# A planned retention and mixture kernel: new durations in its planner, one load on another queue, other bursts and other filler

## The chip, the core and the metric

One Trainium2 chip, of which the kernel uses one core. The metric is the device time of one execution in microseconds (us). Five engines work side by side, each through its own instructions in order: TensorE (PE in the profile, its weight loads PEld), VectorE (DVE), ScalarE (ACT), GpSimd (POOL) and SyncE (SP), which here only issues transfers. An instruction that waits holds up all behind it on its engine.

## The reference

Eight batches of eight heads, 576 positions, 64 values per head. Retention (attention without a softmax, with a decay per head) and then two dense layers with a leaky ReLU between them:

```python
scores = scale * np.matmul(q, k.transpose(0, 1, 3, 2))
gamma = 1.0 - 2.0 ** (-5.0 - np.arange(H, dtype=np.float32))
Dmat = np.where(rel >= 0, gamma[:, None, None] ** rel[None, :, :], 0.0)
attn = np.matmul(scores * Dmat[None], v)
x = attn.transpose(0, 2, 1, 3).reshape(4608, 512)
h = x @ w_in                 # 512 x 2048
out = np.maximum(0.01 * h, h) @ w_out   # 2048 x 512
```

## The kernel before

**Units.** The 4608 tokens are cut into 36 units of 128 tokens, two chunks of 64 each. For unit u, `load` (L619) brings k, q and v as 128 x 8 x 64 float32 (jobs `ld{u}.1`, `.0`, `.2`). `casts` (L641) makes float16: k is copied (`ck`, L648), q and v are multiplied by the decay (`cq`, `cv`: L652 on DVE or POOL, L656 as eight small instructions on ACT). q and k are transposed, for units 0 to 7 by PE with a copy from PSUM (`turn_pe`, L686 and L693), later by a transposing transfer on SP's queue (`turn_dma`, L672).

**Retention.** `inner` (L710) computes the scores within a chunk (`sa`, L721), the mask (`mk`, DVE, L736), the states k^T v (`sb`, L730), their running sums (`st`, DVE, L779 to L785) and the sums in float16 (`sx`, L799 and L802). `outer_mm` (L838) multiplies scores by v (own part) and states by q (cross part) into the PSUM tile `ot` (L842); a copy turns it into x (`x{u}`, L891). All these matmuls are 64 x 64 and run on quarters of the array. They come in three forms: units 0 to 3 (below `drain`) in separate jobs, with a drain of PE between own and cross part (L903); units from 4 to below `joined`, `parted`, as two short bursts (cross part and scores, job `ca{u}`; states and own part, jobs `sb{u}` and `ow{u}`); all later ones as one long burst (`bu{u}`, L755), which also holds the own part of the unit before.

**Dense layers.** Four units make a group of 512 tokens, nine groups. Groups 0 to 2 take layer 1 as it is (`layer1`, L947 with leaky ReLU on ACT, L954); its blocks need quarters of w_in (four loads `wi0` to `wi3`, L921). All others, and layer 2 everywhere, use a scheme of seven products instead of eight (`seven`, L1048, a variant of Strassen's): layer 1 at L1128, layer 2 at L1204, with sums on DVE (L1108 `xs`, L1182 `mix`, L1150, L1237) and copies of PSUM on ACT or DVE (L1073 `cA`, L1078 `u2`, L1081 `k5`). The weights' mixtures (L995, L1024) are formed once on DVE. The output leaves by SP's queue (L1039, L1240).

**What sets the order.** Nothing is issued as it is written. Every step becomes a job with an engine, two durations in ns (how long it keeps the engine, and when its result is there), the jobs it waits for and the buffers it opens. `Plan.order` (L120) then plays the machine on the host: it takes again and again the job that can begin first, among those that can begin within `slack` the one with the earliest due time, and so fixes each engine's order. The durations stand in the table `COST` (L589), in `BURST`, in `SWITCH` (what PE loses at each change between 64 x 64 and full matmuls) and in the `add` calls; when a load lands is modelled, and four early landings are given by hand (`landing`). Which engine takes a copy stands in tables (`engines`, `eng`), and due times are shifted job by job in two more (`nudge`, `shift_due`).

**Filler.** Where the planner sees PE idle before a job, `filler` (L1296) puts matmuls of zeros (`idle`, 512 columns, L1304) into PE's order, counted by the planned length of the gap. They are ordinary instructions: they run whether or not PE is late.

**Loads.** POOL's queue issues units 1 to 11, w_in and w_out; SP's queue unit 12 and later. Unit 0's k and q go by SP, its v by POOL, ahead of w_in. A POOL load takes POOL's own time to issue (about 0.9 us), and a POOL order holds casts as well. In the built order a queue has eight semaphores in turn, so the ninth transfer is issued when the first has landed.

Of the kernel before, what the change touches and what calls it, by code (L numbers as in the profile page):

```python
# [46 lines left out]
class Plan:  # L47
# [3 lines left out]
    SWITCH = 115  # L51
# [68 lines left out]
    def order(self, margin=30, slack=30, filler=None):  # L120
        self.urgency(margin)
        jobs = self.jobs
# [55 lines left out]
        while todo:  # L178
# [12 lines left out]
            if best is None:  # L191
                raise RuntimeError("no job can begin: " + ", ".join(
                    f"{j.name}({','.join(a.name for a in j.after if a.end is None)};{j.follow.name if j.follow and j.follow.start is None else ''})"
                    for j in jobs if j.start is None and (j.name[0] in 'ab')))
# [56 lines left out]
def _cfg():  # L251
# [28 lines left out]
            "cv0 sx0.0 yt2.1 sx2.1 sx3.1 cv4 yt4.0 sx5 sx7 sx11 sx12 cq13 cv16 sx19 sx21 sx25 cq26 cv27 cv30 "  # L280
            "sx30 sx31 sx32 sx35 ",
        "DVE":
# [4 lines left out]
        "POOL":  # L287
            "ck3 cv7 cv8 cq10 cv10 cv11 sx13 cv17 sx18 ck19 ck20 ck24 sx24 ck26 sx27 sx28 ck29 cq29 sx29 ck31 "
            "ck32 cv32 ck33 cv33 sx33 cv34 sx34 cv35 ",
    }  # L290
    nudge = {
        -10026:
            "cv29 ",
        -10724:
            "h0.12.384 ",
        -10966:
            "mk4 ",
        -11853:
            "xs4.2 ",
        -11976:  # L300
            "a3.2.k5 ",
        -12515:
            "b3.21 ",
        -128684:
            "a6.3.p2.0 ",
        -14832:
            "h2.4.256 ",
        -15153:
            "m3.1.0 ",
        -15169:  # L310
            "mk23 ",
        -15592:
            "ld18.0 ",
        -19363:
            "ca4 ",
        -2236:
            "sx3.0 ",
        -251919:
            "cv1 ",
        -2689:  # L320
            "m1.2.1 ",
        -293979:
            "b8.p1.1 ",
        -31306:
            "h0.12.0 ",
        -40696:
            "sx2.0 ",
        -429774:
            "a8.3.p7.0 ",
        -653:  # L330
            "m4.2.0 ",
        -8008:
            "xs5.2 ",
        -837:
            "mk26 ",
        -8459:
            "mk34 ",
        -8774:
            "ld21.2 ",
        -9071:  # L340
            "m3.2.1 ",
        11277:
            "tr22 ",
        12355:
            "st33.0 ",
        14015:
            "ld29.0 ",
        15252:
            "xs7.2 ",
        15629:  # L350
            "mk29 ",
        15684:
            "xs5.3 ",
        18754:
            "ld14.1 ",
        18924:
            "h1.10.256 ",
        21497:
            "m5.0.0 ",
        23022:  # L360
            "b5.p4.0 ",
        28841:
            "ld26.0 ",
        3776:
            "m3.3.1 ",
        3956:
            "mk21 ",
        3958:
            "m3.0.0 ",
        5404:  # L370
            "st32.0 ",
        5601:
            "m3.2.0 ",
        5647:
            "b0.p1.0 ",
        6624:
            "m5.1.1 ",
        7138:
            "x29 ",
        7265:  # L380
            "st24.0 ",
        8339:
            "so2.1 ",
        8675:
            "bu31 ",
    }
    shift_due = {
        -12686:
            "b1.p1.0 b1.p1.1 b1.cA b1.p2.0 b1.p2.1 b1.11 b1.p6.0 b1.p6.1 b1.u2 b1.p5.0 b1.p5.1 b1.k5 b1.p7.0 "
            "b1.p7.1 b1.22 b1.p3.0 b1.p3.1 b1.12 b1.p4.0 b1.p4.1 b1.21 ",  # L390
        -14351:
            "l1.6.0 l1.6.256 ",
        -166113:
            "h2.2.0 h2.2.256 ",
        -16905:
            "b3.p1.0 b3.p1.1 b3.cA b3.p2.0 b3.p2.1 b3.11 b3.p6.0 b3.p6.1 b3.u2 b3.p5.0 b3.p5.1 b3.k5 b3.p7.0 "
            "b3.p7.1 b3.22 b3.p3.0 b3.p3.1 b3.12 b3.p4.0 b3.p4.1 b3.21 ",
        -179758:
            "h1.0.0 h1.0.256 ",
        -20648:  # L400
            "b0.p1.0 b0.p1.1 b0.cA b0.p2.0 b0.p2.1 b0.11 b0.p6.0 b0.p6.1 b0.u2 b0.p5.0 b0.p5.1 b0.k5 b0.p7.0 "
            "b0.p7.1 b0.22 b0.p3.0 b0.p3.1 b0.12 b0.p4.0 b0.p4.1 b0.21 ",
        -26677:
            "l1.4.0 l1.4.256 ",
        -26684:
            "a6.0.p1.0 a6.0.cA a6.0.p2.0 a6.0.11 a6.0.p6.0 a6.0.u2 a6.0.p5.0 a6.0.k5 a6.0.p7.0 a6.0.22 "
            "a6.0.p3.0 a6.0.12 a6.0.p4.0 a6.0.21 ",
        -28444:
            "x16 ",
        -29807:  # L410
            "l3.3.22 l3.3.12 ",
        -30711:
            "a4.2.p1.0 a4.2.cA a4.2.p2.0 a4.2.11 a4.2.p6.0 a4.2.u2 a4.2.p5.0 a4.2.k5 a4.2.p7.0 a4.2.22 "
            "a4.2.p3.0 a4.2.12 a4.2.p4.0 a4.2.21 ",
        -31154:
            "a5.1.p1.0 a5.1.cA a5.1.p2.0 a5.1.11 a5.1.p6.0 a5.1.u2 a5.1.p5.0 a5.1.k5 a5.1.p7.0 a5.1.22 "
            "a5.1.p3.0 a5.1.12 a5.1.p4.0 a5.1.21 ",
        -31278:
            "a7.0.p1.0 a7.0.cA a7.0.p2.0 a7.0.11 a7.0.p6.0 a7.0.u2 a7.0.p5.0 a7.0.k5 a7.0.p7.0 a7.0.22 "
            "a7.0.p3.0 a7.0.12 a7.0.p4.0 a7.0.21 ",  # L420
        -31546:
            "a5.0.p1.0 a5.0.cA a5.0.p2.0 a5.0.11 a5.0.p6.0 a5.0.u2 a5.0.p5.0 a5.0.k5 a5.0.p7.0 a5.0.22 "
            "a5.0.p3.0 a5.0.12 a5.0.p4.0 a5.0.21 ",
        -31652:
            "a4.1.p1.0 a4.1.cA a4.1.p2.0 a4.1.11 a4.1.p6.0 a4.1.u2 a4.1.p5.0 a4.1.k5 a4.1.p7.0 a4.1.22 "
            "a4.1.p3.0 a4.1.12 a4.1.p4.0 a4.1.21 ",
        -36269:
            "a4.0.p1.0 a4.0.cA a4.0.p2.0 a4.0.11 a4.0.p6.0 a4.0.u2 a4.0.p5.0 a4.0.k5 a4.0.p7.0 a4.0.22 "
            "a4.0.p3.0 a4.0.12 a4.0.p4.0 a4.0.21 ",
        -37687:  # L430
            "x27 ",
        -39781:
            "l5.2.22 l5.2.12 ",
        -44863:
            "xs7.0 xs7.1 xs7.2 xs7.3 ",
        -45803:
            "a6.2.p1.0 a6.2.cA a6.2.p2.0 a6.2.11 a6.2.p6.0 a6.2.u2 a6.2.p5.0 a6.2.k5 a6.2.p7.0 a6.2.22 "
            "a6.2.p3.0 a6.2.12 a6.2.p4.0 a6.2.21 ",
        -46221:
            "h0.4.0 h0.4.128 h0.4.256 h0.4.384 ",  # L440
        -53848:
            "l4.3.22 l4.3.12 ",
        -65535:
            "l3.0.22 l3.0.12 ",
        -6965:
            "b7.p1.0 b7.p1.1 b7.cA b7.p2.0 b7.p2.1 b7.11 b7.p6.0 b7.p6.1 b7.u2 b7.p5.0 b7.p5.1 b7.k5 b7.p7.0 "
            "b7.p7.1 b7.22 b7.p3.0 b7.p3.1 b7.12 b7.p4.0 b7.p4.1 b7.21 ",
# [970 lines left out]
```

## Time and profile before

| | |
|---|---|
| median of three runs | 292.39 us (290.34, 292.39, 293.9) |
| the profiled execution | 290.67 us, of which the span from first to last instruction is 288.9 us |
| mean granted PE clock | 0.994 of full speed |
| DMA | 50.08 MB, mean 173 GB/s; share of the 16 engines 1.1 and more in most stretches until 200 us, 0.22 and less from 200 to 270 |
| POOL L652 (multiplies of q and v) | 38, mean 1057 ns (q) and 1125 ns (v) |
| DVE L652 (multiplies of q) | 18, mean 756 ns |
| DVE L1182 (mixtures) | 72, means 682 to 788 ns by form |
| DVE L1150 and L1237 (sums with one operand in PSUM) | 66, means 683 to 688 ns |
| filler matmuls | 36 |

A row of the profile names engine, line, operation, the tile written and the tiles read, the count, and busy time with the mean of one. In a timeline a row begins with its start and length in us; in square brackets stands the idle time just before it and what ended it. A row of the stretches gives the stretch, its length, the busy time of PE, PEld, DVE, ACT and POOL with counts, then the granted PE clock, the DMA share and GB/s. Matmuls overlap, so their lengths add up to more than the time they take: distances from start to start are the better measure.

### The profile page before, as it was taken

What the parts mean: (1) busy time and instruction counts of PE and PEld (TensorE: products, weight loads), DVE (VectorE), ACT (ScalarE), POOL (GpSimd) and SP (SyncE); (2) the same over time, 40 slices, a digit from 0 to 9 for tenths busy, and PEclk for the clock granted to TensorE, in tenths of its full rate; (3) what the DMA queues carried; (4) which work ended last, traced back from release to release, by engine and by line L of the source; (5) the groups of instructions that cost most, each with busy time, mean ns of one, the idle gap of its engine ahead of it and who ended that gap; (6) DMA issues with size and microseconds to landing.
All of it is one profiled execution on the core that took longest, in us unless ns stands there. A gap on an engine that the chain in (4) does not pass through costs nothing.

```text
span 288.9 us, 10486 instructions
## 1 busy us (share of the span) xinstructions
PE 277.2 (96%) x4532; PEld 233.3 (81%) x4532; DVE 215.4 (75%) x385; ACT 182.1 (63%) x366; POOL 94.3 (33%) x111
## 2 busy tenths in 40 slices
PE   8979999999999999999899999999999999999994
PEld 3559978888878888887788888888888888888883
DVE  1575777998986798877998889889958963872541
ACT  3515987543657857775595789778755755566630
POOL 8867996743141233323321412354010000000000
PEclk9989999999999999999999999999999999999999
DMA  7996999999999999999999999999401100300303
GB/s 160 288 233 144 281 209 235 324 196 173 188 278 222 210 197 218 262 205 236 231 223 242 204 269 215 183 221 217 69 3 75 74 2 0 149 0 2 149 0 145
DMA packets 119247, 50.08 MB, mean 173 GB/s; under 512 B 107936, under 2 KB 112672, under 8 KB 119200
## 3 DMA queue, kind: packets, MB, share of 16 engines
q1 hardware_dynamic: 111856, 36.19, 59.9%
q0 software_dynamic: 7056, 13.11, 19.3%
q8 instruction: 35, 0.57, 0.9%
q10 hardware_dynamic: 288, 0.11, 0.2%
q14 instruction: 12, 0.10, 0.1%
HBM read 36.81 MB, written 9.44 MB: 160 GB/s over the span
## 4 chain that ended last, share of the span: by engine, by line
PE 70%; DVE 9%; DMA 9%; SPq 6%; issue 3%; POOL 1%; ACT 1%; ACTq 0%; DVEq 0%; POOLq 0%
PE acc L1204 29%; PE acc L1128 20%; PE acc L947 13%; DMA w_in<-in_moe_w_in_dram 6%; SPq L627 5%; PE ot L842 4%; DMA t<-in_k_dram 2%; DVE s L736 2%; PE sc L730 2%; DMA t<-in_q_dram 1%; DVE w_mix L995 1%; PE sc L721 1%; SPq L672 1%; DVE mix L1182 1%; DVE sum L1150 1%
## 5 line engine op out<-in xcount | busy, mean ns | idle before, releaser
L1204 PEld LDWEIGHTS <-gt 128*128 128x128 f16 x720 | 69.5, 98 | 8.4
L1204 PE MATMUL acc<-w_out,gt 128*128 128x256 f16 x432 | 54.8, 273 | 0.0
L947 PE MATMUL acc<-xT,w_in 128*128 128x128 f16 (+1 forms) x512 | 48.3, 251 | 1.9 <-DMA w_in<-in_moe_w_in_dram 1.3
L947 PEld LDWEIGHTS <-w_in 128*128 128x128 f16 x512 | 40.0, 100 | 5.9 <-issue 1.8
L1128 PEld LDWEIGHTS <-w_in 128*128 128x128 f16 x384 | 36.4, 98 | 7.3 <-issue 2.4
L1155 ACT ACTIVATE gt<-sum 128x512 f16<-128x512 f32 x48 | 29.7, 628 | 19.4 <-DVE sum L1150 19.4
L954 ACT ACTIVATE gt<-acc 128x512 f16<-128x512 f32 x48 | 28.3, 597 | 17.7 <-PE acc L947 17.6
L1146 ACT ACTIVATE gt<-acc 128x512 f16<-128x512 f32 x48 | 28.5, 594 | 13.7 <-PE acc L1128 13.3
L1204 PE MATMUL acc<-w_mix,gt 128*128 128x256 f16 x288 | 36.0, 273 | 0.0
L652 POOL TENSOR_TENSOR v<-t,cs 128x512 f16<-128x512 f32 x22 | 24.7, 1125 | 25.1 <-DMA t<-in_v_dram 10.3
L652 POOL TENSOR_TENSOR qk<-t,cs 128x512 f16<-128x512 f32 x16 | 16.9, 1057 | 48.9 <-PE sc L730 17.5
L736 DVE TENSOR_TENSOR s<-sc,cs 128x512 f16<-128x512 f32 x36 | 24.7, 686 | 9.8 <-PE sc L721 6.6
L1204 PEld LDWEIGHTS <-mix 128*128 128x128 f16 x288 | 27.7, 98 | 4.2 <-issue 0.6
L1128 PEld LDWEIGHTS <-w_sum 128*128 128x128 f16 x288 | 27.6, 98 | 4.1 <-DVE xs L1108 0.8
L1128 PE MATMUL acc<-xs,w_in 128*128 128x256 f16 x192 | 28.9, 273 | 1.0 <-DVE sum L1150 1.0
L1128 PE MATMUL acc<-xs,w_sum 128*128 128x256 f16 x192 | 28.9, 273 | 0.5 <-DVE xs L1108 0.5
L1128 PE MATMUL acc<-xT,w_in 128*128 128x256 f16 x192 | 28.9, 273 | 0.5 <-DVE acc L1073 0.3
L1150 DVE TENSOR_TENSOR sum<-acc,k 128x512 f32<-128x512 f32 x24 | 16.5, 688 | 10.0 <-ACT k L1081 5.9
L1081 ACT COPY k<-acc 128x512 f32<-128x512 f32 x28 | 16.4, 589 | 7.9 <-PE acc L1128 4.1
L781 DVE TENSOR_TENSOR s<-sc,s 128x256 f32<-128x256 f32 x40 | 16.7, 418 | 4.0 <-PE sc L730 2.1
L652 DVE TENSOR_TENSOR qk<-t,cs 128x512 f16<-128x512 f32 x18 | 13.6, 756 | 8.1 <-DMA t<-in_q_dram 7.3
L1073 ACT COPY acc<-acc 128x512 f32<-128x512 f32 x26 | 15.0, 577 | 7.2 <-PE acc L1204 4.0
(68 smaller groups left out, 461.8 us busy)
## 6 DMA issues: line engine op xcount, KB each, us to landing
out_dram<-osb SPq DMA_DIRECT2D x17, 512.0 KB, 4.0
t<-in_k_dram SPq DMA_DIRECT2D x22, 256.0 KB, 4.7
t<-in_q_dram SPq DMA_DIRECT2D x22, 256.0 KB, 4.5
t<-in_v_dram SPq DMA_DIRECT2D x21, 256.0 KB, 4.8
t<-in_v_dram POOLq DMA_DIRECT2D x11, 256.0 KB, 6.3
t<-in_k_dram POOLq DMA_DIRECT2D x10, 256.0 KB, 7.4
t<-in_q_dram POOLq DMA_DIRECT2D x10, 256.0 KB, 6.6
w_in<-in_moe_w_in_dram POOLq DMA_DIRECT2D x8, 256.0 KB, 8.3
```

What stands on the lines that cost most here:

```text
L652: engine[e].tensor_tensor(out=out, in0=t32[u, 2 * x][:], in1=decay(u, x), op=MUL)
L736: landed[u] = nc.vector.tensor_tensor(out=s[:], in0=a[:, :, 0], in1=mask_sb.unsqueeze(1).unsqueeze(1).to_broadcast([P, 2, NP, CH]), op=MUL,)
L781: nc.vector.tensor_tensor(out=to, in0=x, in1=before[0][:, before[1]], op=ADD)
L947: nc.tensor.matmul(out=a[:, n, :], lhsT=w_in16[:, c, (f0 + n) * P : (f0 + n + 1) * P], rhs=x[:, c, t0 : t0 + nt], start=(n == 0 and c == 0 ...
L954: nc.scalar.activation(out=y[:, f0 : f0 + nf, t0 : t0 + nt], in_=a[:], func=mybir.ActivationFunctionType.Lrelu)
L1073: op("cA", ce, lambda: copies[ce](out=B[:], in_=A[:]), [done["1"]], [B], [A], "1")
L1081: op("k5", ke, lambda: copies[ke](out=k5[:], in_=C[:]), [done["5"]], [k5], [C], "5")
L1128: nc.tensor.matmul(out=r[:, f, :], lhsT=w[:, c, (2 * n + f) * P : (2 * n + f + 1) * P], rhs=rhs[:, c, :], start=fresh and c == 0 and f == ...
L1146: w = op(what, "ACT", lambda: nc.scalar.activation(out=to(), in_=r[:], func=lr), after, [y], [r], m)
L1150: what, "DVE", lambda: nc.vector.tensor_tensor(out=s[:], in0=r[:], in1=plus[:], op=ADD),
L1155: lambda: nc.scalar.activation(out=to(), in_=s[:], func=lr), [j], [y], [s],
L1204: nc.tensor.matmul(out=r[:, tb, :], lhsT=lhs[n]()[:, f, tb * P : (tb + 1) * P], rhs=rhs[n][:, f, :], start=fresh and i == 0 and k == 0, st ...
```

## The change

1. *Durations.* `COST` and other durations of the planner are replaced:

```diff
-    SWITCH = 115
+    SWITCH = 97
-        ("ACT", "psum"): (490, 640), ("DVE", "psum"): (603, 735),
+        ("ACT", "psum"): (490, 638), ("DVE", "psum"): (603, 731),
-        ("ACT", "cast"): (540, 670), ("DVE", "mul"): (610, 740), ("POOL", "mul"): (1020, 1250),
-        ("DVE", "cast"): (310, 420), ("DVE", "cast256"): (190, 300), ("ACT", "cast256"): (340, 460),
-        ("DVE", "mix"): (680, 800), ("DVE", "wmix"): (760, 900), ("DVE", "xs"): (345, 460),
-        ("ACT", "f32"): (505, 640), ("ACT", "mul"): (1930, 2050),
+        ("ACT", "seed"): (515, 640), ("DVE", "seed"): (603, 735),
+        ("ACT", "cast"): (519, 660), ("DVE", "cast"): (337, 475), ("POOL", "cast"): (600, 790),
+        ("ACT", "cast256"): (340, 460), ("DVE", "cast256"): (230, 370), ("POOL", "cast256"): (390, 560),
+        ("ACT", "mul"): (1930, 2060), ("DVE", "mul"): (602, 735), ("POOL", "mul"): (1000, 1220),
+        ("DVE", "mix"): (604, 735), ("DVE", "wmix"): (604, 735), ("DVE", "xs"): (337, 475),
+        ("ACT", "f32"): (537, 680),
-    BURST = 590
+    BURST = 562
-                f"bu{u}", "PE", (BURST, BURST + 205), all_,
+                f"bu{u}", "PE", (BURST, BURST + 268), all_,
-            jb = add(f"sb{u}", "PE", (100, 340), sb, ...
+            jb = add(f"sb{u}", "PE", (147, 376), sb, ...
-                f"ca{u}", "PE", (140, 380), ca,
+                f"ca{u}", "PE", (220, 458), ca,
-                f"ow{u}", "PE", (170, 400), own, ...
+                f"ow{u}", "PE", (210, 467), own, ...
-            f"oa{u}", "PE", (530, 760), both, ...
+            f"oa{u}", "PE", (588, 786), both, ...
-        seven("1", f"a{g}.{n}.", mm, 1, 4 * 109.7, due, needs, outs, [x, z])
+        seven("1", f"a{g}.{n}.", mm, 1, 4 * 109.25, due, needs, outs, [x, z])
```

2. *v of unit 0* is issued by ACT's queue (the planner still counts it as a load of SP):

```diff
-        ("u", 0, ("SP", "SP", "POOL")), ("wi", 0), ("u", 1, "POOL"), ...
+        ("u", 0, ("SP", "SP", "ACT")), ("wi", 0), ("u", 1, "POOL"), ...
-        landing={"ld0.1": 3870, "ld0.0": 4970, "ld0.2": 6070, "wi0": 10300}, ...
+        landing={"ld0.1": 3870, "ld0.0": 4970, "ld0.2": 5500, "wi0": 9300}, ...
```

3. *Two short bursts* only for units 4 to 15, with a drain of PE ahead of unit 4's cross part:

```diff
-        ... joined=20,
+        ... joined=16,
             def ca():
+                if not parted(u - 1):
+                    nc.tensor.drain()
                 cross(u - 1 if u - 1 in landed and parted(u - 1) else None)
```

4. *Filler* from 350 instead of 500 ns of planned idling up to 24 us, with more matmuls for the same gap:

```diff
     def filler(free, t):
-        if t - free < 500 or t > CFG["fill_until"]:
+        early = t < CFG["fill_tight"]
+        if t - free < (350 if early else 500) or t > CFG["fill_until"]:
             return None
         a = Buf(acc_pool, [P, 1, TOK], FP, "acc", True)
-        n = max(1, int((t - free - 250) / 225))
+        n = max(1, int((t - free - 50) / 216) if early else int((t - free - 250) / 225))
```

5. *Tables.* `eng`, `nudge` and `shift_due` are replaced whole. With the new tables POOL takes more casts (here the lists of the multiplies of q, `cq`, and casts of k, `ck`, and what stays for DVE):

```diff
-  DVE: cq0 ck4 ck6 cq7 ck9 cq11 ck12 ck13 cq14 cq18 cq20 ck23 cq23 cq24 ck25 ck27 ck28 cq31 cq32 ...
-  POOL: ck3 cq10 ck19 ck20 ck24 ck26 ck29 cq29 ck31 ck32 ck33 ...
+  DVE: cq0 ck3 ck4 ck6 cq7 ck10 cq11 ck13 ck18 cq21 cq26 ck31 ...
+  POOL: ck2 cq2 ck7 ck8 cq9 ck14 ck15 ck16 ck19 cq19 ck21 ck23 ck24 ck25 cq29 ck30 ck32 ck33 ck34 ck35 ...
```

6. The first product of a group's layer 1 is ordered behind the last but one group's layer 2 (`second[g - 2]`), and a switch `chain` decides whether POOL's loads keep their written order; it is on, as the kernel before has it.

What is computed stays the same; every engine's order is a new one.

More of the change, by code (lines that the diff above doesn't have):

```diff
@@ L191, in order @@
             if best is None:
[L192 to L194 removed]
+                raise RuntimeError("no job can begin")
             t, j = best
@@ L312, in _cfg @@
[L312 to L337, printed above, removed]
@@ L403, in _cfg @@
[L403 to L417, printed above, removed]
@@ L616, in x_of, with load_due, follow @@
         return xT[u // 4][:, :, t0 : t0 + P]
+    asked, last = {"SP": 0, "POOL": 0}, {}
+    def load_due(eng):
+        asked[eng] += 1
+        return 1000.0 * asked[eng] - 3000 if eng == "POOL" and not CFG["chain"] else None
+    def follow(j):
+        if j.eng == "SP" or CFG["chain"]:
+            j.follow, last[j.eng] = last.get(j.eng), j
     def load(u, engs):
@@ L906, in outer @@
         j = written[u] = add(
-            f"oa{u}", "PE", (530, 760), both, after + [written.get(u - 1)], [], uses + (waiting[1] if waiting is not None else []), mode="q"
+            f"oa{u}", "PE", (588, 786), both, after + [written.get(u - 1)], [], uses + (waiting[1] if waiting is not None else []), mode="q"
         )
```

537 lines of the change are left out of this document (373 added, 164 removed), and 10 rows, old and new, of tables (eng, loads).

## The prediction

> **What bounds the kernel now.** I read the page's busy shares and slices first, then the busy time by stretch, the chain that ended last, TensorE's timeline, and last the timelines of VectorE (DVE) and GpSimd (POOL) where TensorE (PE) stands still.
>
> ```profile
> PE 277.2 (96%) x4532; PEld 233.3 (81%) x4532; DVE 215.4 (75%) x385; ACT 182.1 (63%) x366; POOL 94.3 (33%) x111
> PEclk9989999999999999999999999999999999999999
> ```
>
> PE is the bound, but "busy" counts overlapping matmuls and filler, so I count its work by start-to-start distances. Back to back, a 256-column matmul takes 109.3 ns (in the chain, 24 take 2.62 us), a 128-column one 56 ns (16 take 0.89 us). That is 1936 x 109.3 ns + 256 x 56 ns = 225.9 us of dense products, and 64 transposes x 56 ns = 3.6 us. The 64x64 attention matmuls come in blocks between dense ones. What a block adds is the distance from the dense matmul before it to the one behind it, less one dense step:
>
> ```profile
> 93.72 1.04 PE L1204 MATMUL acc<-w_mix,mix 128*128 128x256 f16 x8
> ...
> 95.00 1.05 PE L947 MATMUL acc<-xT,w_in 128*128 128x256 f16 x8
> 95.89 1.04 PE L1204 MATMUL acc<-w_out,mix 128*128 128x256 f16 x8
> ...
> 97.31 1.05 PE L1204 MATMUL acc<-w_out,mix 128*128 128x256 f16 x8
> ```
>
> A block of 24 adds 95.00 - 93.72 - 8 x 0.109 = 0.41 us, a block of 40 adds 97.31 - 95.89 - 0.87 = 0.55 us. One of 64, in the next answer, adds 161.94 - 160.73 - 0.44 = 0.77 us:
>
> ```profile
> 160.73 0.60 PE L1128 MATMUL acc<-xs,w_sum 128*128 128x256 f16 x4
> ...
> 161.94 0.61 PE L1128 MATMUL acc<-xs,w_in 128*128 128x256 f16 x4
> ```
>
> All three fit 0.197 us per block plus 9.05 ns per matmul. Before has 58 blocks with 2240 matmuls: 31.7 us. Useful PE work is 225.9 + 3.6 + 31.7 = 261.1 us of a 288.9 us span. The other 27.8 us, by subtracting useful work from each stretch: 15.5 until 20.2 us (filler and idling while the first loads come), 1.3 from 20.2 to 23.4, 0.7 until 40, then 6.4 in the middle, of which 5.5 us stand in seven places of 0.35 us and more (1.0 at 40 to 43, 0.6 at 61, 0.7 at 85, 1.9 at 135 to 142, 0.5 at 150, 0.5 at 194, 0.35 at 226), and 3.9 us behind the last matmul. Only these can shrink, and the block count.
>
> The start:
>
> ```profile
> 1.23 5.51 PE L1304 MATMUL acc<-idle 128*128 128x512 f16 x14 [1.23 <-DVE idle L586]
> ...
> 8.60 1.04 PE L1304 MATMUL acc<-idle 128*128 128x512 f16 x4
> 9.56 0.32 PE L730 MATMUL sc<-v,qk 64*64 64x64 f16 x16
> ...
> 18.39 0.55 PE L721 MATMUL sc<-qkT 64*64 64x64 f16 x16 [0.47 <-DVE qkT L693]
> 20.22 3.26 PE L947 MATMUL acc<-xT,w_in 128*128 128x128 f16 x32 [1.28 <-DMA w_in<-in_moe_w_in_dram]
> ...
> 26.82 1.96 PE L947 MATMUL acc<-xT,w_in 128*128 128x128 f16 x32
> ```
>
> ```profile
> 12.20:20.20 8.00, 5.83 (x135) 3.92 (x135) 6.23 (x15) 2.94 (x6) 5.56 (x8) 0.96 1.16 240
> 20.20:23.40 3.20, 3.18 (x32) 3.11 (x32) 0.91 (x3) 0.89 (x2) 2.04 (x4) 0.56 1.00 207
> ```
>
> PE waits for the second quarter of w_in until 20.2, DMA being full from 5.9 on (share 1.07 and 1.16). Then the granted clock is 0.56 for 3.2 us: 32 matmuls take 3.26 us, which take 1.96 at full clock. Filler runs in PE's order too: the four at 8.60 are over only when L730 starts.
>
> The largest stop in the middle, in the timelines of DVE, POOL and PE:
>
> ```profile
> 137.54 0.43 DVE L648 CAST qk<-t 128x512 f16<-128x512 f32 x1 [0.66 <-DMA t<-in_k_dram]
> ...
> 139.41 1.55 DVE L1182 TENSOR_TENSOR mix<-gt 128x1024 f16<-128x1024 f16 x1
> ...
> 142.08 0.68 DVE L1182 TENSOR_TENSOR gt<-gt 128x1024 f16<-128x1024 f16 x1
> ```
>
> ```profile
> 138.37 1.04 POOL L652 TENSOR_TENSOR qk<-t,cs 128x512 f16<-128x512 f32 x1 [4.10 <-ACT u L1078]
> 139.37 1.04 POOL L652 TENSOR_TENSOR v<-t,cs 128x512 f16<-128x512 f32 x1
> ```
>
> ```profile
> 141.62 0.60 PE L1128 MATMUL acc<-xs,w_in 128*128 128x256 f16 x4 [1.02 <-DVE sum L1150]
> ```
>
> DVE first stands in its own order behind a load that is late (0.66), then its two-input operation takes 1.55 instead of 0.68 us while POOL multiplies; PE waits for the sum queued behind.
>
> **The change, part by part.** How the new tables move instructions I took from the two built orders, PE's, DVE's, ACT's, POOL's and SP's. All times below are against the profiled execution: 290.67 us, span 288.9.
>
> *Blocks.* Units 16 to 19 get one burst instead of two short ones; the new order has 54 blocks, the matmuls are the same. 4 x 0.197 = **-0.8** us. Bounds: -0.8, and -0.2 if three of the four were in a wait anyway. PE ran without gaps at 86 to 135, where such blocks stand, so -0.8.
>
> *A drain* before unit 4's cross products. The same instruction stands behind the own products of units 0 to 3 (L903); in the chain of waits it shows as 0.11 and 0.13 us of "issue" (at 23.80 and 29.35), and the matmuls on its two sides start 0.25 to 0.29 further apart than without it. **+0.25**, bounds 0 and +0.3.
>
> *v of unit 0 on ACT.* Its issue stands behind the warm-up activation, which ends at 3.14, and takes about 0.45 (the row of the constants on ACT's queue); ACT's next, the cast of k, starts at 3.72, so ACT pays nothing. k and q needed 3.0 and 4.0 us from issue to use, so v is there at 6.1 to 7.1, before: 6.7. Its eight multiplies (2.02) end at 8.1 to 9.1. The first transposed q now sits behind them on ACT (0.6 more) and S^T behind that, but PE comes later still (next part): cost 0; if that cover went, up to 0.7. POOL is rid of 1.05 us of issue (1.27 to 2.33), so all its loads can start up to 1.05 earlier, w_in included; with DMA full, the bytes ahead of the second quarter stay the same. Landing 19.1 to 20.1. POOL also gets k and q casts and a state copy ahead of w_in's third quarter: before its issue 15.16, now after the first states, some 18 us. Before, it landed at 25.8 and was used at 27.8; the queue ahead of it is still full then, and its use comes at about 26: 0, at worst +0.8.
>
> *More filler.* 50 instead of 35 of them stand ahead of the matmuls that need the second quarter. PE then cannot reach these before: 1.23 (start) + 11 x 0.427 + 39 x 0.216 + 4.7 of useful work + two drains 0.5 = 19.6 us (the first row of the start above is eleven at 0.427 and three at 0.216: the first transposes start at 6.57). Before, the same sum gives 16.3 and 3.9 us of idling to 20.22. So filler replaces nearly all idling, and unit 0 itself gets later: the first L947 block needs 36 fillers ahead instead of 28 and cannot come before 13.2 (before: 12.17). The start of the second quarter's matmuls is the later of 19.6 and 19.1 to 20.1: I take 19.8, **-0.4**, bounds -0.65 and +0.5. The clock: the slow stretch followed one in which PE idled; with PE full until 19.6 I take the clock at 1.00: 3.26 - 1.96 = **-1.3**, the other end 0. On this the Trainium skill, page "TensorE: Matmul & The Clock Gate", section "HAM oscillation", says that a re-throttle needs an idle gap of more than about 3.4 us. Here the clock fell with no gap over 1.28, so the trace does not bear it out as a rule for gaps; by it the filler would buy nothing here and the sum be 1.3 higher.
>
> *The reordering of the middle.* In the new order DVE has 9 fewer multiplies of q (18 to 9, 0.76 each = -6.8 us), 7 more full state copies (0.42), 2 more copies from PSUM (0.69), 4 fewer casts or transposed copies (0.42) and 2 fewer half copies (0.45): -5.0 us, and 11 fewer instructions that wait for a load in DVE's order. POOL gets 8 more multiplies (1.06 to 1.13), 7 more casts (0.67) and one more state copy net: +13 us, so 74 operations, not 58, that can hit DVE. Overlength on DVE is about 9 us now (the surplus of the means of L1182, L995, L1024, L652 and L785 over their shortest forms); a quarter more POOL time makes about +2. Net, DVE is freer by some 3 of 215 us. Stops on PE: I take 5.5 down to 4.3, **-1.2**; ends: -3.5 (only the first and the last place stay) and +7 (eight more collisions of 0.87). Near the better half because both things that made the stop at 141 get rarer or no worse on DVE, but every instruction has moved. ACT loses 4 us of 182, nothing on the path. The tail (last product, two half copies, two stores) is the same: 0.
>
> Sum: -0.8 + 0.25 - 0.4 - 1.3 - 1.2 = -3.4, so 287.2 us for an execution like the profiled one. That one lies 1.7 below the median 292.39, and the four times shown (290.34, 290.67, 292.39, 293.9) have a mean 1.1 above it; I put the forecast at 287.2 + 1.1 = **288.3**, the same 1.1 added below.
>
> **The rivals.**
> (a) *The filler is only paid for.* The quarter lands at 20.1, and the middle stops as often as before: 290.7 - 0.8 + 0.25 - 0.1 + 1.1 = 291.1 with the clock lost again. For it: DMA is full from 5.9, and each hundred ns by which the planned filler overshoots delays the units. Against: 3.9 us of idling.
> (b) *The clock falls anyway*, all else as forecast: 289.6. This is also what the page's rule on gaps would give.
> (c) *POOL's extra work becomes the wait: slower.* Each collision costs DVE 0.87 (1.55 - 0.68), and from 120 to 200 DVE has little room. Blocks, drain, start and clock give 2.25; three collisions on the path eat that, six and more make it slower by 1%. At eight: 290.7 - 2.25 + 7 + 1.1 = 296.5. For: 16 more POOL operations. Against: DVE does 5 us less. The Trainium skill, page "SBUF — State Buffer", section "Who interferes with whom", says that a DVE operation with two SBUF inputs and a reading GpSimd operation block each other whole. The rows above agree (1.55 for 0.68 beside 1.04).
> (d) *DVE's relief clears the middle:* stops down to 2.0: 286.0.
>
> **Chances and range.** Forecast 0.45, (a) 0.18, (b) 0.12, (c) 0.10, (d) 0.15. One per cent, about what a measurement of this kernel tells from no change, is 2.9 us: the line is 289.5. Faster: 0.38 of the forecast's, all of (d), 0.05 of (b): 0.58. Slower (over 295.3): 0.07 of (c), 0.02 of (a)'s tail: 0.09. Same: 0.33. Range 284.8 (d with its own 1.2 below) to 292.2 (a with its tail): about 0.13 is left out. The forecast's own range: 286.5 to 290.
>
> **What would show it.** Right: a clock of 1.00 in every slice, the L947 block after 32 or more filler at about 13.2, the second quarter's first matmul between 19.4 and 20.1, 54 blocks, idling over 0.3 us in the middle summing to 3 to 5 us, DVE busy near 212. Wrong: a granted clock of 0.5 behind 19 us (b), L1182 means above 0.80 with PE waiting for DVE sums or mixes (c), a wait for w_in's third quarter at 26 us, or a new stop over 2 us anywhere.

## The result, and the profile after

The changed kernel takes 305.39 us (median of 302.79, 308.65, 305.53, 305.25), the kernel before, timed beside it, 293.14 (290.34, 292.39, 293.9, 294.24). The ratio is 1.040, 95% interval 1.029 to 1.052: slower, where 288.3 was forecast. Ratios leave out executions more than 1.5% over the fastest of their kernel; single times of one kernel scatter by 2 to 4% here, so small differences below rest on profiles.

The profiled execution took 302.79 us (span 301.0, before 288.9). Busy shares, granted clock and DMA by slice on the page of after:

```profile
PE 283.0 (94%) x4547; PEld 235.4 (78%) x4547; DVE 214.2 (71%) x379; ACT 179.6 (60%) x363; POOL 106.2 (35%) x126
...
PEclk9959999799999999999999999999999999999999
DMA  7950999993799999999999999999931200200303
```

The clock is halved in the third slice and lowered in the eighth, and DMA, whose share is 1.10 from 5.9 to 12.2 us and 0.94 from 12.2 to 20.2, stands still in the fourth slice (22.6 to 30.1 us). Useful PE work, counted as for before, is 260.35 us (261.14). So 40.65 us are lost now, 27.8 before. By stretches: 25.6 up to 30 us (17.4 before), 5.3 from 30 to 60 (1.2), 5.8 from 60 to 275 (5.0); 8.2 + 4.1 + 0.8, less 0.8 of blocks and 0.2 in the tail, is the 12.1 us of span.

**The start.** After's timelines of PE, ACT, DVE and POOL, and two stretches (busy times with counts, granted clock, DMA share, GB/s):

```profile
10.42 0.40 PE L866 MATMUL acc<-ident,qk 128*128 128x128 f16 x4 [2.74 <-DVE qk L832]
...
16.80 1.93 PE L910 MATMUL sc<-v,qk 64*64 64x64 f16 x16 [4.47 <-ACT v L836]
...
23.63 1.05 PE L1129 MATMUL acc<-xT,w_in 128*128 128x128 f16 x16
...
30.70 2.84 PE L1129 MATMUL acc<-xT,w_in 128*128 128x128 f16 x48
```

```profile
1.65 1.28 ACT L752 ACT_TABLE_LOAD   x1 [1.65 <-PEq L1581]
1.71 0.47 ACTq L805 DMA_DIRECT2D t<-in_v_dram  x1
...
16.40 2.02 ACT L836 ACTIVATE v<-t,cs 128x64 f16<-128x64 f32 x8 [11.95 <-DMA t<-in_v_dram]
```

```profile
9.67 0.69 DVE L832 TENSOR_TENSOR qk<-t,cs 128x512 f16<-128x512 f32 x1 [8.50 <-DMA t<-in_q_dram]
```

```profile
28.59 0.40 POOL L982 CAST st<-s 128x256 f16<-128x256 f32 x1 [11.37 <-DVE s L961]
28.93 1.31 POOL L1103 DMA_DIRECT2D w_in<-in_moe_w_in_dram  x2
```

Before, v and q were used here:

```profile
6.73 2.02 ACT L656 ACTIVATE v<-t,cs 128x64 f16<-128x64 f32 x8 [2.39 <-DMA t<-in_v_dram]
```

```profile
5.25 0.69 DVE L652 TENSOR_TENSOR qk<-t,cs 128x512 f16<-128x512 f32 x1 [4.08 <-DMA t<-in_q_dram]
```

After's two stretches:

```profile
12.20:20.20 8.00, 3.41 (x32) 1.56 (x35) 0.72 (x2) 2.48 (x9) 4.93 (x6) 0.70 0.94 234
20.20:23.40 3.20, 3.11 (x47) 1.28 (x44) 1.91 (x4) 0.41 (x1) 0.00 (x0) 0.67 0.01 3
```

v of unit 0 is issued at 1.71, even earlier than forecast (the issue does not wait for the table load), but it is there only at 16.4: ACT stands for 11.95 us. q, which SP issues as before, is used at 9.67 instead of 5.25. PE waits 2.74 and 4.47 us and fills the rest with zeros; the first block of layer 1 starts at 23.63 (12.17 before), the second quarter's matmuls at 30.70 (20.22). The clock is halved from 15.5 to 22.3. POOL's order now has a state copy ahead of w_in's third quarter; that copy hangs on the same v, so the quarter is issued at 28.93 (15.16 before), and DMA empties (share 0.01).

What v met on the way stands in the DMA queues' packets from 4 to 16 us (packets, MB, share of 16 engines; q0 is POOL's queue, q10 ACT's, q1 SP's):

```profile
q0 software_dynamic: 1437, 2.52, 93.1%
q10 hardware_dynamic: 1040, 0.26, 11.3%
q1 hardware_dynamic: 556, 0.14, 6.3%
```

POOL's 1437 packets carry 1.75 KB on the mean (by the trace's packet sizes, w_in's are of 1 KB and those of units 1 and 2 behind it of 4 KB), the 1596 of the other two 256 bytes. Over the whole stretch POOL's queue and the other two together sent about as many packets each, and so v and q got a seventh of the bytes. Within it the counts are not equal: from 7 to 7.5 us ACT's queue has 222 packets and POOL's 42, from 12 to 12.5 us ACT's 11 and POOL's 50. By 9.5 us all but 170 of v's packets had gone; these last ones took another 6 us.

**The stop at 50 us.** PE's timeline, and the queues from 49 to 52 us:

```profile
50.18 0.20 PE L910 MATMUL sc<-v,qk 64*64 64x64 f16 x4
52.22 0.29 PE L910 MATMUL sc<-v,qk 64*64 64x64 f16 x12 [1.84 <-ACT gt L1136]
...
52.90 4.45 PE L1129 MATMUL acc<-xT,w_in 128*128 128x256 f16 x24
```

```profile
q0 software_dynamic: 573, 0.57, 118.8%
q8 instruction: 1, 0.02, 2.0%
```

PE stops for 2.0 us, and the clock is halved behind that (24 matmuls in 4.45 us, 2.62 at full clock). The bracket names ACT, but the stop lies inside one job of sixteen matmuls, four of which had run. What did come just ahead is the single 16 KB packet of the queue named "instruction", from 49.86 to 50.84. The experiments come back to it.

**The middle.** After's largest stop behind 60 us is at 159.7 (1.4 us). PE waits for ACT to copy a product out of PSUM, and in ACT's order that copy stands behind a cast of k whose load is late; ACT had stood idle for 2.08 us. After's PE and ACT:

```profile
161.08 0.60 PE L1310 MATMUL acc<-xT,w_sum 128*128 128x256 f16 x4 [1.23 <-ACT k L1263]
```

```profile
159.93 0.62 ACT L828 CAST qk<-t 128x512 f16<-128x512 f32 x1 [2.08 <-DMA t<-in_k_dram]
160.46 0.58 ACT L1263 COPY k<-acc 128x512 f32<-128x512 f32 x1
```

DVE's mixtures do still run long beside POOL's multiplies (L1366 takes 1.52 us at 156.94, beside 1.48 us of POOL L832 from 156.43), but PE's stop here has another cause. It is like the first half of what was shown at 141 before: an engine that stands in its own order behind a late load.

### The profile page after: what moved, and what is told of

It is laid out like the page before. It is cut to its first block, busy times and chain, and to the rows that moved or that the text cites. A ratio compares the mean times of both kernels' runs of the same rounds, so it can differ in the third digit from the quotient of the medians.

```text
span 301.0 us, 10519 instructions
## 1 busy us (share of the span) xinstructions
PE 283.0 (94%) x4547; PEld 235.4 (78%) x4547; DVE 214.2 (71%) x379; ACT 179.6 (60%) x363; POOL 106.2 (35%) x126
## 4 chain that ended last, share of the span: by engine, by line
PE 71%; DMA 15%; SPq 4%; DVE 3%; ACT 2%; issue 1%; POOL 1%; ACTq 0%; POOLq 0%
PE acc L1388 30%; PE acc L1310 19%; PE acc L1129 12%; DMA t<-in_v_dram 5%; DMA t<-in_q_dram 4%; DMA t<-in_k_dram 4%; PE ot L1024 3%; PE sc L910 2%; PE acc L1489 2%; SPq L805 2%; DMA qkT<-qk 2%; PE sc L901 2%; SPq L852 2%; DVE w_mix L1177 1%; PE acc L866 1%
## 5 line engine op out<-in xcount | busy, mean ns | idle before, releaser
L832 POOL TENSOR_TENSOR qk<-t,cs 128x512 f16<-128x512 f32 x22 | 23.9, 1085 | 47.5 <-DMA t<-in_q_dram 29.2
L1388 PE MATMUL acc<-w_mix,gt 128*128 128x256 f16 x288 | 36.7, 273 | 0.0
L1310 PEld LDWEIGHTS <-w_sum 128*128 128x128 f16 x288 | 27.8, 98 | 4.8 <-issue 1.2
L832 POOL TENSOR_TENSOR v<-t,cs 128x512 f16<-128x512 f32 x24 | 26.7, 1114 | 12.6 <-DMA t<-in_v_dram 8.9
L1388 PEld LDWEIGHTS <-mix 128*128 128x128 f16 x288 | 27.8, 98 | 4.3 <-issue 0.8
L1263 ACT COPY k<-acc 128x512 f32<-128x512 f32 x27 | 15.9, 589 | 10.0 <-PE acc L1310 5.5
L1255 ACT COPY acc<-acc 128x512 f32<-128x512 f32 x29 | 16.7, 577 | 7.0 <-PE acc L1388 5.6
L982 POOL CAST st<-s 128x256 f16<-128x256 f32 x6 | 3.2, 534 | 48.4 <-DVE s L965 32.4
```

The costliest lines, as they stand in the source:

```text
L832: engine[e].tensor_tensor(out=out, in0=t32[u, 2 * x][:], in1=decay(u, x), op=MUL)
L1255: op("cA", ce, lambda: copies[ce](out=B[:], in_=A[:]), [done["1"]], [B], [A], "1", COST[ce, "seed"])
L1263: op("k5", ke, lambda: copies[ke](out=k5[:], in_=C[:]), [done["5"]], [k5], [C], "5")
L1310: nc.tensor.matmul(out=r[:, f, :], lhsT=w[:, c, (2 * n + f) * P : (2 * n + f + 1) * P], rhs=rhs[:, c, :], start=fresh and c == 0 and f == ...
L1388: nc.tensor.matmul(out=r[:, tb, :], lhsT=lhs[n]()[:, f, tb * P : (tb + 1) * P], rhs=rhs[n][:, f, :], start=fresh and i == 0 and k == 0, st ...
```

## The experiments

My theory from these lines: v on ACT's queue goes in packets of 256 bytes, with POOL's w_in now beside instead of behind it, and loses the race for the DMA engines. The rival: longer filler, POOL's casts and the new orders hold up the start.

**1. v back on POOL's queue, all else of the change kept.**

```diff
-        ("u", 0, ("SP", "SP", "ACT")), ...
+        ("u", 0, ("SP", "SP", "POOL")), ...
-        landing={... "ld0.2": 5500, "wi0": 9300}, ...
+        landing={... "ld0.2": 6070, "wi0": 10300}, ...
```

> The changed kernel with one part undone: v of unit 0 goes by POOL's queue again, ahead of w_in, with its two planned landings (6070 and 10300) as before; all else of the change stays. Theory: after lost its start because v and q of unit 0, in the hardware queues' packets of 256 bytes, fall behind w_in, which POOL's queue sends at the same time; in after v landed at 16.3 us and q at 9.6. With v first in POOL's own queue nothing of w_in competes: v lands at 6.4 to 7.2, q at 4.9 to 5.6, the first block of layer 1 starts at 12.5 to 14, the second quarter's matmuls at 19.4 to 21, and the time is 290 +- 3 us. Rival: the start is held up by the longer filler and by POOL's casts and state copy ahead of w_in's third quarter; then the first block still comes after 18 us and the time stays above 297.

Median 295.54 (288.24 to 299.69, 6 executions), before 293.96 (289.04 to 296.15, 11). ACT's and PE's timelines:

```profile
6.51 2.02 ACT L836 ACTIVATE v<-t,cs 128x64 f16<-128x64 f32 x8 [1.89 <-DMA t<-in_v_dram]
```

```profile
13.46 1.05 PE L1129 MATMUL acc<-xT,w_in 128*128 128x128 f16 x16
...
20.11 2.84 PE L1129 MATMUL acc<-xT,w_in 128*128 128x128 f16 x48
24.44 0.51 PE L1129 MATMUL acc<-xT,w_in 128*128 128x128 f16 x6
25.89 0.73 PE L1129 MATMUL acc<-xT,w_in 128*128 128x128 f16 x10 [0.94 <-issue]
```

The start is what the prediction drew (13.2, 19.8, clock 1.00), and some 9 us are back. But the kernel is not faster than before; a second loss is left, and its first piece is the 0.94 us in the last line, in the middle of a block, with nothing to wait for.

**2. After with v on SP's queue.**

```diff
-        ("u", 0, ("SP", "SP", "ACT")), ...
+        ("u", 0, ("SP", "SP", "SP")), ...
```

> The changed kernel with v of unit 0 as the third load of SP's queue in place of ACT's; all orders otherwise as in after. Theory (small packets of a hardware queue beside w_in, whichever engine issues them): v still lands late, after 12 us, and the time is within 3 us of after's. Rival (something of ACT's queue, such as the transfer being issued while the activation table is loaded): v lands at 7 us or earlier and the time is near 290.

307.4 us (306.57, 308.24). ACT's queue is not the cause:

```profile
17.17 2.02 ACT L836 ACTIVATE v<-t,cs 128x64 f16<-128x64 f32 x8 [12.63 <-DMA t<-in_v_dram]
```

**3. The kernel before, with only v on ACT's queue.**

```diff
-        ("u", 0, ("SP", "SP", "POOL")), ...
+        ("u", 0, ("SP", "SP", "ACT")), ...
-        landing={... "wi0": 10300}, ...
+        landing={... "wi0": 9300}, ...
```

> The kernel before with one part of the change alone: v of unit 0 on ACT's queue, w_in's planned landing 1 us earlier; durations, bursts, filler rule and tables stay as before. Theory: v lands after 13 us, q after 8, and the time is 9 to 13 us over before's. Rival (the loss comes from the other parts, filler above all, or only together with them): v lands by 8 us and the time is within 2 us of before's.

302.04 (300.12 to 303.2), before 293.96: ratio 1.034, 1.022 to 1.047. The time grows by 8.1 us, a little under what I expected, and v is used as late as in after:

```profile
16.64 2.02 ACT L657 ACTIVATE v<-t,cs 128x64 f16<-128x64 f32 x8 [12.02 <-DMA t<-in_v_dram]
```

This one edit does most of the harm.

**4. v on ACT's queue, and POOL issues w_in only when it has multiplied v.**

```diff
+    eng["ACT"] = eng["ACT"].replace("cv0 ", ""); eng["POOL"] = "cv0 " + eng["POOL"]
-        landing={... "ld0.2": 5500, "wi0": 9300}, ...
+        landing={... "ld0.2": 6600, "wi0": 14500}, ...
+    w_in_job[0].after.append(cast[0, 2])
```

> The changed kernel with v of unit 0 on ACT's queue, as in after, but POOL multiplies v first and issues w_in only behind that, so that nothing of w_in can run beside v. Theory: v lands at 5.5 to 7 and q at 4.9 to 5.6, though both go by the same queues as in after; w_in's first quarter lands 3 to 5 us later than in after, the second at 22 to 25, and the time is 293 to 299 us, well under after's. Rival (v on ACT's queue is slow by itself): v lands after 12 us with w_in out of its way, and the time is above after's 305.

295.99 (295.0, 296.99). POOL:

```profile
6.50 1.04 POOL L833 TENSOR_TENSOR v<-t,cs 128x512 f16<-128x512 f32 x1 [6.05 <-DMA t<-in_v_dram]
7.48 1.44 POOL L1104 DMA_DIRECT2D w_in<-in_moe_w_in_dram  x2
```

The same queue brings v in 4.8 us (1.70 to 6.50) when only k and q of the same unit run beside it. w_in is issued 6.2 us later than in after, DMA stands still from 6.1 to 8.8 us, and the kernel is still 9 us faster than after. (POOL now multiplies v in ACT's place, and the planner's orders are new, so the time alone would not show the cause; the landing does.)

**5. v as 128 rows of 2 KB, in after** (other values of the same tensor: unit 0's result is not that of the reference).

```diff
+                if eng == "ACT":
+                    engine[eng].dma_start(
+                        out=t[0:P], in_=v[0, 0:2].rearrange("h (a t) d -> (h a) t d", t=8)[0:P]
+                    )
+                    return
```

> The changed kernel with v of unit 0 still on ACT's queue, but read as 128 rows of 2 KB that lie together (other values of the same tensor, so unit 0's result is not that of the reference) in place of 1024 rows of 256 bytes. Theory (the hardware queue loses because its packets are small beside POOL's of 1 to 3 KB): v lands by 9 us, the first block of layer 1 starts before 15 and the time is 291 to 297. Rival (a hardware queue loses to POOL's queue whatever its packets are): v still lands after 12 us and the time is within 4 us of after's 305.

298.41 (296.42, 300.41); the first block of layer 1 starts at 14.83. ACT's use of v, and the queues from 4 to 16 us:

```profile
9.26 2.02 ACT L841 ACTIVATE v<-t,cs 128x64 f16<-128x64 f32 x8 [4.72 <-DMA t<-in_v_dram]
```


```profile
q0 software_dynamic: 1417, 2.52, 95.9%
q10 hardware_dynamic: 143, 0.26, 6.5%
q1 hardware_dynamic: 526, 0.13, 5.3%
```

The same bytes in an eighth of the packets, on the same queue beside the same w_in, land 7 us earlier. So v is late neither for its bytes nor for its queue, but because it goes in many small packets beside POOL's loads. The Trainium skill, page "DMA: Bandwidth & Descriptors", section "Queues, rings and completion order", says that each DMA engine takes the queues in turn, a whole packet from one before it switches. This case agrees in that v's landing followed the size of its packets, and in after's sum (1437 packets of POOL's queue in the time of 1596 of the other two). After's shorter stretches (222 to 42, 11 to 50) do not show equal turns; the trace does not tell the DMA engines apart, and no run shows that the profile's packets are the page's, which hold several descriptors each. How the engines share, and what held v's last 170 packets, stays open. The time is slightly over what I expected: the profile has three stops like that of 24.4 us above, 0.4 to 2.4 us long.

**The second loss.** I numbered PE's instructions in order of time (weight loads, matmuls, and PE's few drains and semaphore rows), and set the last one ahead of each stop beside the 16 KB packets of the instruction queue. Some of the rows (times in us; the number is the last instruction ahead of the stop):

```
kernel   PE instruction   PE stops     PE goes on   packet           its end to "goes on"
before   449 + 256 x 4    41.50        42.36        39.99 to 40.94   1.43
after    449 + 256 x 4    50.19        52.22        49.86 to 50.84   1.38
1        449 + 256 x 1    24.73        25.89        23.49 to 24.44   1.45
1        449 + 256 x 2    30.93        32.13        29.66 to 30.60   1.53
1        449 + 256 x 4    42.69        43.88        41.36 to 42.33   1.55
4        449 + 256 x 1    28.81        29.70        27.33 to 28.22   1.48
```

Of PE's stops in the sixteen profiles of this study, 24 (0.3 to 2.4 us from start to start) stand at 449 + 256 k, with k from 1 to 4, and each ends 1.21 to 1.62 us behind such a packet, whatever matmul it is. The page of after counts 35 such packets, and its 4547 matmuls and as many weight loads are 35.5 times 256. My reading is that PE has run out of instructions: the next 256 come by the same DMA engines as the loads, and from 20 to 55 us, with DMA full, they come late. After's 2.0 us at 50 is one of them. The Trainium skill, page "Runtime: NRT & Kernel Launch", section "Instruction fetch mechanics", gives blocks of 16 KB with 256 instructions, as the trace has them, and calls a refill's cost mostly hidden. By that such stops would hardly show; here they take 0.9 us of before and 3.5 of kernel 1.

**6. Kernel 1 with the old rule of filler.**

```diff
-        if t - free < (350 if early else 500) or ...
+        if t - free < 500 or ...
-        n = max(1, int((t - free - 50) / 216) if early else int((t - free - 250) / 225))
+        n = max(1, int((t - free - 250) / 225))
```

> The changed kernel with v of unit 0 back on POOL's queue, and with the old rule of filler (from 500 ns, one matmul per 225 ns after 250). Against the kernel that differs only in the rule (294.6 us profiled; second quarter's matmuls from 20.11, clock 1.00 throughout), by the forecast's step: PE idles 3 us or more before the second quarter, the granted clock falls to 0.5 to 0.6 for some 3 us about 19 to 24 us, and that costs 1 to 2 us there. Rival (the filler is only paid for): the clock stays at 1.00 or the loss up to 24 us is no larger than with the new rule. The time lies within 3 us of that kernel's either way.

295.16 (291.62 to 299.11, 10). A miss: with 39 filler instead of 51 the second quarter's matmuls start at 20.09, the clock stays at 1.00 until 44.8, and 15.6 us are lost up to 24 us with both rules. In the new orders the rule gains nothing. From 24 to 60 us it has three refill stops (0.55, 1.52, 2.31 us), the longest with 3.4 us of half clock behind it.

**7 and 8. Before with the new rule of filler (the diff of 6 the other way round), and that with two short bursts to unit 15 only.**

```diff
-        ... joined=20,
+        ... joined=16,
```

> The kernel before with the changed filler rule alone. By the forecast's step: second quarter's matmuls from 19.4 to 20.3, clock 1.00 there, and 0.8 to 1.7 us less lost up to 24 us than before. Behind that: where PE stops in the middle of a block with no wait for a semaphore, it does so at PE instruction 449 + 256 k and 1.4 to 1.55 us behind the end of a 16 KB instruction packet (theory: a refill of PE's instructions that comes late because DMA is full); such stops are expected once to three times between 20 and 55 us, of about 1 us each, in place of one of 0.87 before. Time: -1.5 +- 3 against before. Rival for the stops: their places by instruction number differ from kernel to kernel with the order, as a wait for data would.

> The kernel before with the changed filler rule and two short bursts for units 4 to 15 only (durations, queues and tables as before). By the forecast's terms: blocks 58 to 54 (-0.8), start and clock (-0.4 and -1.3): 2 to 2.5 us under before if nothing new stops PE. Rival: the orders that the planner makes anew with tables that were made for another setting bring 2 to 5 us of new stops in the middle, and the time is not below before's.

299.32 (298.69 to 304.34; ratio 1.029, 1.022 to 1.036) and 299.47 (296.85 to 300.9; 1.025, 1.019 to 1.031). Up to 24 us they lose 15.5 and 16.2 us (before 17.0), the clock is 1.00 there, and neither has a refill stop, against what I expected. From 60 to 275 us they lose 14.0 and 13.6 us, before 5.0. The planner's orders are new there, with hand-set due times made for the old ones. PE's waits in 7 are spread over many causes; the two largest, over the whole execution (us in total, times, longest):

```profile
PE ot L842 <- POOL st L799: 2.6, 3, 1.1
PE acc L1128 <- DVE sum L1150: 1.6, 2, 1.2
```

**9. Before with its orders kept, and only the emitted filler of the new rule** (`n` still goes into the plan, the job emits more).

```diff
+        more = max(n, int((t - free - 50) / 216)) if t < 24000 else n
-            for _ in range(n):
+            for _ in range(more):
```

> The kernel before with every order as it was planned; only the filler jobs up to 24 us emit the changed rule's count, 49 filler matmuls in place of 36. This separates the filler from the new orders that the planner makes when the rule itself is changed (that kernel took 2.9% longer than before, with its first 60 us 1.5 us shorter). Theory: the second quarter's matmuls start at 19.8 to 20.3 with the clock at 1.00, 1.2 to 1.8 us less is lost up to 24 us, and the middle stops as before, so the time is 1 to 2 us under before's. Rival (filler is only paid for): no less is lost up to 24 us, and the time is the same or more.

292.66 us (289.54 to 296.03 and one execution of 463.46; 12), before 293.8 (288.28 to 298.6 and one of 353.13; 23); ratio 1.004, 0.999 to 1.009: no difference. Up to 24 us 0.94 us less is lost, and the clock holds; the matmuls come at 20.6, later than I expected. From 24 to 60 us 6.1 us are lost (1.5 before): refill stops of 0.43 and 1.18, and 3.4 us of half clock behind them. The 26 added PE instructions had moved the places where PE can run dry. Behind 60 us it loses 3.3 us (5.0 before) with the same orders.

**10. Kernel 1 with 90 PE instructions more at the start, in the same time** (the first filler job in matmuls of 128 columns).

```diff
-            for _ in range(n):
+            for _ in range(n if free > 2000 else 0):
...
+            for i in range(4 * n if free <= 2000 else 0):
+                nc.tensor.matmul(
+                    out=a[:, 0, 0:P], lhsT=idle[:, 0:P], rhs=idle[:, 0:P], start=True, stop=True
+                )
```

> The changed kernel with v of unit 0 on POOL's queue (294.6 us profiled, with stops of PE at 24.7, 30.9 and 42.7 us), whose first filler job is cut into four times as many matmuls of 128 columns, which take the same time: 90 PE instructions more ahead of everything else, all orders the same. Theory (PE waits for a refill of 256 instructions that comes late): the stops now lie at other matmuls, 90 instructions earlier in the program, and each again at PE instruction 449 + 256 k, 1.4 to 1.6 us behind the end of a 16 KB instruction packet; together 2 to 5 us between 20 and 55 us. Rival (PE waits for data at these matmuls): the stops stay at the same matmuls, which are then instructions 283 + 256 k.

291.10 (289.31 to 295.9, 8), before 293.8; ratio 1.001, 0.995 to 1.008. Half a miss: there is no stop at 449 + 256 k at all, where I expected them moved. But PE also runs through the matmuls at which kernel 1 stopped (24.44 and 25.89 above), so they were not waiting for data.

**11. Kernel 1 with POOL's two state copies and two casts ahead of w_in's third quarter taken off POOL.**

```diff
-            "sx1.0 sx1.1 ck2 cq2 ck7 cv7 ck8 ...
+            "ck7 cv7 ck8 ...
```

> The changed kernel with v of unit 0 on POOL's queue, and with the state copies of unit 1 and the casts of k and q of unit 2 taken off POOL (they go to the engines that have them by default), so that nothing but loads and the casts it had before stands ahead of w_in's third quarter. Theory: the third quarter is issued at 14.5 to 16 (18.3 with them), the DMA share of 12 to 20 us rises from 0.83 to over 1.0, the loads behind it no longer come in one heap from 18 to 24 us, a refill of PE's instructions then takes under 6 us from 20 to 33 us, and the stops at 24.7 and 30.9 (1.2 us each) go or shrink to under 0.5; the time is 1 to 4 us under the 295 of the kernel with them, if the planner's new orders add no stops in the middle. Rival (the place of these casts costs nothing, as the forecast had it): the stops of 20 to 33 us stay over 1.5 us together.

299.91 (296.01 to 301.4, 4). The quarter is issued at 15.86 (18.33 in kernel 1), the DMA share from 12 to 20 is 1.10 (0.83), and of the refill stops up to 37 us 0.83 and 0.32 are left (1.15 and 1.20). But from 24 to 60 us as much is lost as in kernel 1 (5.1 and 5.2), and the new orders lose 12.4 us from 60 to 275. Inconclusive for the copies.

**12 to 14. Kernel 1 with 30, 90 and no instructions more, on one chip.** 13 is 10 again, 14 is 1 again; 12 is 10 with

```diff
-            for i in range(4 * n if free <= 2000 else 0):
+            for i in range(2 * n if free <= 2000 else 0):
-                    out=a[:, 0, 0:P], lhsT=idle[:, 0:P], rhs=idle[:, 0:P], ...
+                    out=a[:, 0, 0:256], lhsT=idle[:, 0:P], rhs=idle[:, 0:256], ...
```

> The changed kernel with v of unit 0 on POOL's queue, whose first filler job is cut into twice as many matmuls of 256 columns: 30 PE instructions more ahead of everything else, the same time, all orders the same. Theory (late refills of PE's instructions): from 20 to 55 us PE has one to three stops of 0.3 us or more at PE instruction 449 + 256 k, that is at matmuls 30 instructions earlier in the program than without the cut, each resumed 1.2 to 1.6 us behind the end of a 16 KB packet, together 1 to 4.5 us; time 291 to 297. Rival (the 90 instructions helped by something else, such as narrower filler): no such stop again, and the time is near 291.

> The same kernel as the one with 90 PE instructions more, timed against before and against the one without them on one chip. Theory: it lies 2 to 5 us under the one without (291.7 and 295.0 in the means so far), and 0 to 2.5 us under before. Rival: the difference was one of chips or of executions, and the two agree within 1 us.

> The changed kernel with v of unit 0 on POOL's queue once more, for the comparison with the shifted ones on one chip. Theory: 293 to 297 us, 2 to 5 over the one with 90 instructions more; in its profile again two or three stops at PE instruction 449 + 256 k from 20 to 55 us. Rival: within 1 us of it.

With 30: 296.68 (2 executions), stops of 0.91 and 0.35 us at 449 + 256 x 1 and x 4, now at other matmuls, as the theory of late refills had it. With 90: 293.81 median, mean 293.9 (12), one stop of 0.38. Without: 297.48 median, mean 298.1 (6), stops of 1.07 and 1.97. Before: 294.3, mean 293.6 (17). The places, at 41 us in 14 and in 13:

```profile
41.48 1.06 PE L1129 MATMUL acc<-xT,w_in 128*128 128x128 f16 x16
42.47 0.32 PE L1024 MATMUL ot<-s,v 64*64 64x64 f16 x16
42.62 0.23 PE L1024 MATMUL ot<-qkT,st 64*64 64x64 f16 x8
42.68 0.20 PE L910 MATMUL sc<-v,qk 64*64 64x64 f16 x4
43.88 0.29 PE L910 MATMUL sc<-v,qk 64*64 64x64 f16 x12 [1.00 <-ACT xT L1073]
```

```profile
40.24 1.06 PE L1129 MATMUL acc<-xT,w_in 128*128 128x128 f16 x16
41.23 0.32 PE L1024 MATMUL ot<-s,v 64*64 64x64 f16 x16
41.37 0.23 PE L1024 MATMUL ot<-qkT,st 64*64 64x64 f16 x8
41.44 0.30 PE L910 MATMUL sc<-v,qk 64*64 64x64 f16 x16
```

Nothing but 90 instructions of filler lies between the two programs, and 4.2 us of their means (standard error 1.4). The refill stops are by the profiles only a part of that. They shrink from 3.0 to 0.4 us, but PE's loss from 24 to 60 us only from 4.0 to 3.6 (from 5.2 to 3.6 between 1 and 10), because other waits stand there instead: 1.10 us for a running sum of DVE in 13, 0.52 for w_in and 0.58 for DVE in 10. Another 1.6 us (2.4 between 1 and 10) are gained behind 60 us, where I found no refill stop. That PE stopped for late refills rests on the places, on the packets and on kernel 12; that they are the whole difference is not shown.

With the 90 instructions the changed kernel, v mended, is even with before (ratio 1.003, 0.995 to 1.010); without them it is slower (1.016, 1.009 to 1.023). No version here is shown to beat before.

## Why the prediction was wrong, step by step

The useful work and the losses of PE in the profiles, in us:

| kernel | useful | lost to 24 | 24 to 60 | 60 to 275 |
|---|---|---|---|---|
| before | 261.1 | 17.0 | 1.5 | 5.0 |
| after | 260.3 | 22.1 | 8.8 | 5.8 |
| 1 / 14 (v on POOL) | 260.3 | 15.6 / 15.9 | 5.2 / 4.0 | 7.5 / 8.3 |
| 10 / 13 (and 90 instructions) | 260.3 | 15.8 / 15.8 | 3.6 / 3.6 | 5.1 / 6.7 |

- **Blocks, -0.8:** right; 54 blocks, 260.35 for 261.14. The drain (+0.25) was not measured alone; nor were the new durations and tables.
- **v of unit 0 on ACT: this step failed.** "k and q needed 3.0 and 4.0 us from issue to use, so v is there at 6.1 to 7.1 ... cost 0". Those 3.0 and 4.0 us were measured with v, not w_in, first on POOL's queue. The edit itself took that shield away. v needed 14.7 us, q 8.4, and the cost is 8 to 9 us: +8.1 in before (3), and 305.4 against a median of 296.2 over the 12 executions of kernels 1 and 14. I asked what POOL's earlier loads do to w_in ("the bytes ahead of the second quarter stay the same", and they do), not what they do to v and q. No rival held it; the slow one, (c), was another mechanism.
- **w_in's third quarter:** issued at "some 18 us" was right with v mended (18.33), and in after wrong by the same v (28.93).
- **Filler and clock, -0.4 and -1.3:** the size is nearly right with v mended: 20.11 for 19.8, clock 1.00, 1.1 to 1.4 us less lost to 24 us. But that is luck, not the filler: in these orders the old rule does as well (6). In the kernel before, the filler brings 0.9 up to 24 us with the orders kept (9) and 1.5 with new ones (7), and neither is faster.
- **The middle, -1.2:** wrong in sign. With v mended 5.1 to 8.3 us are lost behind 60 us, before 5.0. DVE is freed as forecast (214.2 us busy, "near 212") and the means of the mixtures (L1366, L1182 before) are 728 to 782 ns, so (c)'s sign of over 0.80 did not come; the stops moved rather than went. Behind 60 us kernels 1, 10, 13 and 14 wait longest for transposing transfers of q and k (1.0 to 2.1 us in each kernel) and for DVE's mixtures of w_out (0.8 to 1.3); before has 0.4 of the second and none of the first.
- **Left out of the sum altogether:** the refills of PE's instructions, 3.5 and 3.0 us in kernels 1 and 14 against 0.9 in before; with 90 instructions more they go (10) or shrink to 0.4 (13). Before's profile held one of them (41.50), which I had counted as a stop like others. How much of the time they are worth stays open (12 to 14).

What stays open: why a refill comes late in one program and not in another (in 10 and 13 they came in time, by luck of where the 256 fell as far as the runs tell), and what of the middle is due to which order.

## What to carry to other kernels

A load's landing time is a property of what else is under way: an edit that moves a load to another queue also removes its place in the old one, so ask what the old queue sends in the freed time, and in how many packets each load goes. A small load with short rows that PE waits for first belongs ahead of the large ones in their own queue, or the large ones behind its landing. And where PE stops in the middle of a job, count its instructions before believing the releaser that the profile names.

## What the runs showed of the hardware

- 262 KB of v on ACT's queue took 4.8 us from issue to use with POOL's loads held back (4), 7.6 beside them in 128 packets of 2 KB (5), and 14.7 beside them in 1024 of 256 bytes (after); on SP's queue 15.3 (2).
- PE's instructions come by DMA, by all signs here 256 in a packet of 16 KB. 24 times in sixteen profiles, with DMA full, PE stopped behind instruction 449 + 256 k (k from 1 to 4) and went on 1.21 to 1.62 us behind a packet's end. Between 20 and 55 us that cost 0 to 4.4 us.
- Half clock came in multiples of 3.41 us (3.41, 6.83, 10.24): behind a stop of 2.03 us in after, but not behind one of 1.97 in 14, and in before with no gap over 1.28. No run settles what sets it off.
